# A convolution and a two-layer SiLU network on one Trainium2 core: the written-out order of a block, its table of PSUM banks and the list of the first blocks are laid out anew

## The chip, the core and the metric

The kernel runs on one NeuronCore of a Trainium2 chip. TensorE (PE) multiplies matrices into PSUM, which has eight banks of 128 x 512 float32. VectorE (DVE) and ScalarE (ACT) work on vectors, GpSimd (POOL) issues accumulating DMAs, and SyncE (SP) issues the other DMAs. The metric is the time of one execution on the device in microseconds. The kernel before takes 2326.64 us, the median of three runs (2324.93 to 2326.81).

## The reference, cut to what matters

```python
def _attn_ref(x, weight):                  # x: (8, 4096, 192), weight: (8, 7)
    w = softmax(weight, axis=-1)           # seven taps for each of 8 heads
    x_pad = concatenate([zeros((B, 6, D)), x], axis=1)
    x_unf = x_pad[:, idx, :].reshape(B, S, K, H, group)
    out = np.einsum('hk,bskhg->bshg', w, x_unf)   # causal convolution along S
    return out.reshape(B, S, D)

def _moe_ref(x, w_in, w_out):              # x: (32768, 192)
    h = x @ w_in                           # 192 -> 2048
    g = h * (1.0 / (1.0 + np.exp(-h)))     # SiLU
    return g @ w_out                       # 2048 -> 192
```

All of it is float32.

## The kernel before, in words

The 32768 tokens are cut into 32 blocks of 1024 (b = 0 to 31). Each block goes through these steps, and the kernel's text has a token for each:

- Loading and convolution, one block or two ahead. `ld.k` loads x (SP), `i.k` transposes it (DVE), `ha.0` sets the six columns of the block before (POOL and an SP DMA), `v.ki` is tap i of the channels k. Tap 0 is one ScalarE operation. For blocks above 3, each further tap is a ScalarE operation into a `u` buffer and a POOL DMA that adds it into `nat`; for blocks 1 to 3 it is one VectorE operation (line 517). `sp.k` copies the result into `dup` (SP), and `w.i` forms sums of it in `win` (DVE).
- The up stage. The first matrix product is done by a scheme with fewer multiplications than the plain one. `Pr.g` is product r (0 to 14) of group g (0 to 4), one matmul of 64 rows (line 650). The array is split into two halves of 64 rows, e=0 and e=1, and each product belongs to one half. `L.nk` are a few plain products (line 667). Between them a bank is read and written: `uo.g` copies a bank to a `u` buffer (ACT, line 699), `X`, `a` and `b` add or subtract (DVE, line 693), and `S` is the SiLU (ACT, line 711). So a product often waits for a copy or an add of a product a little earlier.
- The down stage. `t.ji` forms differences of SiLU outputs (DVE, 128 x 1024, line 734; t.j1 needs t.j0, t.j3 needs t.j1). `Di.je` is a slot: four matmuls of 32 columns side by side (line 766), for form i (0 to 5), hidden part j (0 to 3), half e. D0 and D1 read SiLU outputs alone; D2 also needs t.j1; D3 needs t.j2 and t.j3; D4 needs t.j0 and t.j3; D5 needs t.j3.
- The end of a block. `x`, `y`, `z` copy accumulators out of PSUM (ACT), `M` adds them (DVE), `o` transposes (DVE), `st` stores (SP).

The order of all this is written out in lists, and every engine does its instructions in the order of the list. `PLAN` holds the 300 tokens of one turn. A token's prefix says which block it is for: none for block b, `-` for b-1, `=` for b-2, `+` for b+1. (Loading and convolution tokens act on the block after the one so named.) PLAN is run for b = 3 to 33. `START` is one longer list that runs first and does the rest of block 0, and blocks 1 and 2; in it `dp` is the plain down stage of block 0 (line 787), `cp` its copies, and `go` starts GpSimd's combining of weights.

The banks are given by tables with rows for block 1, block 2 and all later blocks: `CHAIN_BANKS`, `XBANKS`, `PLAIN_BANKS` for the up stage, `ACC` for the accumulators of the down stage (one for each form 0 to 5; the seventh entry is for the second half of form 3 in the last block), and `DOWN_BANKS` for block 0.

In the last block, tokens in `held` are not done from the list: the t and D tokens of j = 2 and 3, and all of the end of the block. `finish()` does them afterwards in an order of its own. The t and D tokens of j = 0 and 1 are still done in PLAN's order.

`u` buffers are ten, handed out oldest-freed first; a convolution's buffer is free again when its DMA has landed. `t` tiles and the output tile share three buffers, and SiLU outputs have eight.

Of the kernel before, what the change touches and what calls it, by code (L numbers as in the profile page):

```python
# [17 lines left out]
def kernel(  # L18
# [60 lines left out]


    PLAN = (
# [20 lines left out]
    )  # L102
    START = (
# [41 lines left out]
    )  # L145
    QUEUE = (0, 4, 1, 2, 3)
    CHAIN_BANKS = (
# [3 lines left out]
    )  # L151
    XBANKS = (
# [3 lines left out]
    )  # L156
    PLAIN_BANKS = (
        (3, 4, 5),
        (7, 2, 1),
        (6, 1, 3),  # L160
    )
    ACC = (
        (3, 6, 4, 1, 5, 7, 5),
        (0, 3, 1, 2, 4, 6, 5),
        (6, 2, 3, 1, 4, 0, 5),
    )

    def pin(ins):
        return tc.keep_in_program_order(ins)
# [37 lines left out]
    x0 = x.flatten_outer_dims()[TB - pad : TB, :].rearrange("t (k c) -> c k t", k=NK)  # L207
# [565 lines left out]
                )  # L773
            )

    DOWN_BANKS = (7, 0, 2)

    def down_plain(b):

        cmbs[b] = [xpool.tile([P, 4, TB], F32, tag="cmb", name="cmb")]  # L780
        for j in range(NJ):
            for a in range(2):
                for e in range(2):
                    for k in range(NK):
                        for n in range(2):
                            pin(
                                nc.tensor.matmul(  # L787
                                    banks[DOWN_BANKS[k]][R * n : R * n + R, :],
                                    wo[j][:, a, e, R * k : R * k + R],
# [14 lines left out]
    def copy_plain(b, k):  # L804
        pin(nc.scalar.copy(cmbs[b][0][:, k, :], banks[DOWN_BANKS[k]]))

# [329 lines left out]
```

## Time and profile before

| what | value |
|---|---|
| median of 3 runs | 2326.64 us |
| profiled execution | 2326.81 us, its span 2325.1 us |
| PE, share of the span busy | 100% |
| DVE | 76% |
| ACT | 65% |
| POOL | 23% |
| granted clock of PE, mean | 0.999 |

"Busy" is the time in which an engine has at least one instruction under way, as the profiler records it. The stages alternate: an up stage, then a down stage, each about half of a block's time. A chain of waits is followed back from the last instruction; a piece such as "PE ps L766 x384" is a stretch in which it stays on matmuls of line 766. One matmul of float32 shows as two records, two passes, so 384 records are 192 matmuls, the 48 slots of a block. In the lists of instructions an entry in square brackets is the idle time of the engine before the instruction and what ended it.

### The profile page before, as it was taken

How to read it: one execution, taken by the hardware profiler on the slowest of the kernel's cores; microseconds unless marked ns; L12 is line 12 of the kernel's file. 1: busy time of each engine (PE TensorE's matmuls, PEld its weight loads, DVE VectorE, ACT ScalarE, POOL GpSimd, SP SyncE). 2: the span in 40 equal slices, each digit the busy share in tenths (PEclk: the TensorE clock that was granted, in tenths of full speed). 3: DMA queues.
4: the chain of work that ended last, by engine and by line, in shares of the span. 5: the costliest groups of instructions: out<-in, count | busy, mean ns of one | idle time of the engine just before them, and what ended most of it. 6: DMA issues, size and time to landing. Idle time of an engine off the chain costs nothing.

```text
span 2325.1 us, 45494 instructions
## 1 busy us (share of the span) xinstructions
PE 2315.7 (100%) x17630; PEld 978.7 (42%) x17630; DVE 1776.7 (76%) x2373; ACT 1505.4 (65%) x2779; POOL 535.9 (23%) x672
## 2 busy tenths in 40 slices
PE   9999999999999999999999999999999999999998
PEld 4344444344444344444444344444334453344443
DVE  8998877777777778777777777787777777777766
ACT  5347666677666676666776666766667766677642
POOL 4921122212122211222121221112221222212100
PEclk9999999999999999999999999999999999999999
DMA  7324566756566565666565675656666556756501
GB/s 159 67 53 87 100 103 114 126 103 113 91 121 120 105 112 96 112 114 122 103 109 94 119 125 101 116 94 115 114 118 107 102 98 119 123 102 107 88 16 18
DMA packets 523832, 238.80 MB, mean 103 GB/s; under 512 B 431648, under 2 KB 436768, under 8 KB 523616
## 3 DMA queue, kind: packets, MB, share of 16 engines
q0 software_dynamic: 73024, 133.73, 33.8%
q1 hardware_dynamic: 447392, 101.78, 24.3%
q8 instruction: 138, 2.26, 0.4%
q10 hardware_dynamic: 3200, 0.39, 0.1%
q14 instruction: 78, 0.64, 0.1%
HBM read 31.46 MB, written 25.17 MB: 24 GB/s over the span
## 4 chain that ended last, share of the span: by engine, by line
PE 99%; DVE 0%; ACT 0%; issue 0%; ACTq 0%
PE ps L766 48%; PE ps L650 45%; PE ps L667 2%; PE ps L787 2%; PE ps L589 2%; PE ps L1035 1%; PE ps L436 0%; DVE t L734 0%; DVE g L693 0%; DVE cmb L176 0%; ACT u L176 0%; DVE osb L176 0%; PE ps L462 0%; DVE zeros L176 0%; ACTq L969 0%
## 5 line engine op out<-in xcount | busy, mean ns | idle before, releaser
L513 POOL DMA_DIRECT2D nat<-u x504 | 430.9, 917 | 1556.7 <-ACT u L512 539.6
L650 PE MATMUL ps<-win,wr 64*128 64x512 f32 x1550 | 716.3, 591 | 0.0
L766 PE MATMUL ps<-g,wo 128*32 128x512 f32 x2976 | 677.1, 593 | 0.0
L650 PE MATMUL ps<-win,ws 64*128 64x512 f32 x1550 | 636.9, 592 | 0.0
L766 PE MATMUL ps<-t,wo 128*32 128x128 f32 (+2 forms) x4528 | 518.2, 447 | 0.0
L699 ACT COPY u<-ps 128x512 f32<-128x512 f32 x775 | 442.2, 589 | 117.1 <-PE ps L650 87.6
L766 PE MATMUL ps<-t,wx 128*32 128x512 f32 x2976 | 495.4, 592 | 2.2 <-DVE t L734 2.2
L512 ACT ACTIVATE u<-xt,taps 128x512 f32<-128x512 f32 x504 | 347.1, 724 | 166.1 <-DMA nat<-u 165.6
L734 DVE TENSOR_TENSOR t<-g 128x1024 f32<-128x1024 f32 x248 | 302.4, 1220 | 175.6 <-PE ps L766 175.6
L650 PE MATMUL ps<-dup,wr 64*128 64x512 f32 x868 | 422.5, 590 | 0.0
L734 DVE TENSOR_TENSOR t<-g,t 128x1024 f32<-128x1024 f32 x248 | 303.2, 1223 | 112.6 <-PE ps L766 106.1
L650 PEld LDWEIGHTS ps<-win,wr 64*128 64x128 f32 x1550 | 284.8, 187 | 201.6 <-issue 179.0
L711 ACT ACTIVATE g<-ps 128x512 f32<-128x512 f32 x465 | 268.1, 599 | 114.8 <-PE ps L650 106.7
L650 PEld LDWEIGHTS ps<-win,ws 64*128 64x128 f32 x1550 | 264.2, 186 | 163.9 <-issue 93.8
L693 DVE TENSOR_TENSOR g<-u,ps 128x512 f32<-128x512 f32 x465 | 309.3, 676 | 5.6 <-PE ps L650 5.3
L711 ACT ACTIVATE g<-g 128x512 f32<-128x512 f32 x465 | 277.9, 630 | 8.2 <-DVE g L693 8.2
L829 ACT COPY yx<-ps 32x512 f32<-32x512 f32 x150 | 86.9, 579 | 296.3 <-PE ps L766 294.9
L693 DVE TENSOR_TENSOR ps<-u,ps 128x512 f32<-128x512 f32 x310 | 211.8, 692 | 83.2 <-ACT u L699 62.4
L650 PE MATMUL ps<-dup,ws 64*128 64x512 f32 x682 | 269.8, 590 | 0.0
L766 PEld LDWEIGHTS ps<-t,wo 128*32 128x32 f32 x4528 | 179.6, 110 | 204.5 <-issue 201.3
L766 PE MATMUL ps<-g,wx 128*32 128x512 f32 x1488 | 246.6, 595 | 0.0
L766 PEld LDWEIGHTS ps<-g,wo 128*32 128x32 f32 x2976 | 170.9, 110 | 148.5 <-issue 139.1
(92 smaller groups left out, 1952.7 us busy)
## 6 DMA issues: line engine op xcount, KB each, us to landing
nat<-u POOLq DMA_DIRECT2D x504, 256.0 KB, 4.2
dup<-nat SPq DMA_DIRECT2D x345, 128.0 KB, 2.4
nat<-in_x_dram SPq DMA_DIRECT2D x382, 64.0 KB, 3.6
out_dram<-osb SPq DMA_DIRECT2D x376, 64.0 KB, 2.0
raw<-in_moe_w_out_dram SPq DMA_DIRECT2D x8, 384.0 KB, 4.0
raw<-in_moe_w_in_dram SPq DMA_DIRECT2D x12, 192.0 KB, 4.5
ws<-wr POOLq DMA_DIRECT2D x8, 192.0 KB, 5.0
raw<-in_moe_w_in_dram SPq DMA_DIRECT2D x6, 128.0 KB, 3.0
```

Of the source, the lines that this page charges most:

```text
L512: pin(nc.scalar.activation(z, src, AF.Copy, scale=tap))
L513: pin(nc.gpsimd.dma_start(out=dst, in_=z, accum_op=ALU.add))
L589: nc.tensor.matmul(hs[a, n, e], rows(wr[j], e)[:, a, k, :], rows(d, e)[:, n, k, :], start=k == 0, stop=k == NK - 1,)
L650: nc.tensor.matmul(to[:, cols], raw(g, *LEFT[e][r], e), rhs[:, cols], start=first, stop=True, skip_group_check=True,)
L667: nc.tensor.matmul(plain_bank(b, n and 1 + e)[:, cols], rows(wr[j] if own == e else ws[j], e)[:, a, k, :], rows(dups[b], e)[:, SLOT[e][2 * ...
L693: pin(nc.vector.tensor_tensor(out_, u, v, op=op))
L699: pin(nc.scalar.copy(us[b, g, o][:, cols], t1[:, cols]))
L711: pin(nc.scalar.activation(h, src, AF.Silu))
L734: pin(nc.vector.tensor_tensor(t[i // 2][:, i % 2, :], u, v, op=ALU.subtract))
L766: nc.tensor.matmul(accs[b][at][SQ * q : SQ * q + SQ, to], lhs[:, e, SQ * k : SQ * k + SQ], rhs[:, e, ts(q, TB // 4) if i == 5 else to], st ...
L787: nc.tensor.matmul(banks[DOWN_BANKS[k]][R * n : R * n + R, :], wo[j][:, a, e, R * k : R * k + R], gs[b, j, a][:, n, e, :], start=j == 0 an ...
L829: pin(nc.scalar.copy(to, acc[3 * (name[0] == "x") + k][n:P, :]))
```

## The change

PLAN has the same 300 tokens in another order, and the turn is cut at another place: 143 tokens now belong to the block before instead of 114, three (`o.2`, `st.2`, `st.3`) to the block before that, and `v.00`, `v.20`, `v.21` to the block after. START is written anew to fit, 549 tokens instead of 581. The rows of the bank tables for blocks 1 and 2 are new, and of those for all later blocks some entries. Nothing else changes; no function is touched. Cut to the places named below:

```diff
     PLAN = (
-        "+ld.1 -P14.3 -S3.3 -sp.0 -S4.3 P5.0 -P8.2 v.00 v.01 -a1.3 -S1.3 -S1.2 -b5.3 v.20 -t.00 "
-        "-P8.3 -a0.3 -t.02 P5.4 -S0.1 -D1.20 -sp.2 -D1.21 -S5.1 -t.01 -t.03 u5.0 -D1.10 -D0.31 "
-        "-D1.31 v.21 -D2.01 -D1.00 -a0.2 -D3.00 -D3.01 -D2.00 u5.4 -D4.00 -D5.00 v.10 v.11 "
...
+        "+ld.1 -P0.2 -u1.2 -X4.2 -P7.2 -P11.2 -S4.2 =o.2 =st.2 -a1.1 -S1.1 -P0.3 -P12.2 -X4.3 "
+        "-P7.3 v.01 -P11.3 -P12.3 -a5.2 -P4.2 -P14.2 -S4.3 -u1.3 -b1.2 -P10.2 -a5.3 -P8.1 -S5.0 "
+        "-S1.0 -a1.2 -S3.2 -P4.3 v.10 -P8.2 -P14.3 -S3.3 -b1.3 -a1.3 -P10.3 P5.4 -S5.1 v.11 "
+        "-P8.3 P5.0 v.02 -D1.00 =st.3 -t.00 -b5.3 -a0.2 -a0.3 -sp.2 -D1.30 u5.4 -a0.1 -D1.01 "
+        "v.22 v.12 -D0.00 -S0.3 v.23 -D0.31 -D1.10 -t.01 -t.03 -D2.00 -sp.0 -b5.2 -t.02 -D4.01 "
+        "-S1.2 -S5.2 -D5.00 -D2.01 v.03 -D5.01 -D3.00 -S0.1 -t.10 -D1.20 -D4.00 v.13 v.24 "
...
+        "-x2.1 -w.5 -x2.2 -D3.20 -x0.0 -D4.31 -D4.30 -M6.0 -M2.0 L.00 v.16 -M3.0 -M4.0 P2.0 "
+        "u4.0 P5.1 +i.1 L.10 u5.1 L.02 -M5.0 -o.3 -x1.0 P3.0 P6.0 u2.0 X2.0 P2.4 u4.4 -o.0 L.01 "
+        "SL.0 L.12 L.11 SL.1 +ld.0 P1.0 u0.0 SL.2 P9.0 P6.4 u2.4 P13.0 S2.0 X4.0 -M7.0 -st.0 "
+        "+i.0 P2.1 P3.4 X2.4 u4.1 P0.0 u1.0 P7.0 a5.0 P12.0 P11.0 S4.0 b1.0 P1.4 u0.4 P9.4 X4.4 "
+        "P4.0 P13.4 a1.0 P14.0 P10.0 b5.0 P7.4 a5.4 P0.4 S2.4 +ha.0 +v.00 S3.0 P6.1 P8.0 P3.1 "
+        "u1.4 u2.1 P11.4 a0.0 X2.1 P12.4 P4.4 a1.4 +v.20 b1.4 S4.4 S0.0 +v.21 P5.2 u5.2 P14.4 "
...
     START = (
...
+        "-D2.30 -x2.1 v.03 -x2.3 P2.0 u4.0 P3.0 -w.5 L.02 P2.4 u4.4 v.12 v.13 v.14 P6.0 u2.0 "
+        "v.15 v.25 v.26 v.04 -M1.0 -M2.0 -y2.0 L.00 +ld.0 -M6.0 L.01 SL.0 X2.0 P6.4 u2.4 -D4.30 "
+        "-D3.20 -D3.30 -M3.0 -x0.0 -D4.31 -x1.0 P9.0 P1.0 u0.0 -o.0 P13.0 S2.0 X4.0 P1.4 u0.4 "
...
     CHAIN_BANKS = (
-        ((1, 2, 4, 6, 6), (7, 0, 5, 1, 0), (6, 7, 7, 4, 5)),
-        ((2, 6, 5, 4, 0), (4, 0, 6, 1, 3), (1, 2, 3, 0, 7)),
-        ((5, 2, 5, 6, 7), (0, 4, 0, 3, 3), (1, 7, 1, 2, 0)),
+        ((4, 1, 2, 7, 7), (3, 4, 6, 5, 5), (1, 3, 3, 1, 0)),
+        ((0, 2, 5, 4, 6), (1, 6, 1, 0, 7), (5, 3, 2, 3, 0)),
+        ((5, 2, 5, 6, 7), (0, 4, 0, 3, 3), (1, 7, 2, 1, 1)),
     )
...
     ACC = (
-        (3, 6, 4, 1, 5, 7, 5),
-        (0, 3, 1, 2, 4, 6, 5),
-        (6, 2, 3, 1, 4, 0, 5),
+        (1, 2, 7, 4, 3, 5, 7),
+        (3, 4, 6, 1, 0, 2, 7),
+        (0, 6, 1, 3, 4, 2, 7),
     )
...
-    DOWN_BANKS = (7, 0, 2)
+    DOWN_BANKS = (0, 1, 5)
```

More of the change, by code (lines that the diff above doesn't have):

```diff
@@ L147 @@
     CHAIN_BANKS = (
[3 rows of a table removed]
[3 rows of a table added]
     )
     XBANKS = (
[3 rows of a table removed]
[3 rows of a table added]
     )
     PLAIN_BANKS = (
-        (3, 4, 5),
-        (7, 2, 1),
-        (6, 1, 3),
+        (0, 2, 1),
+        (5, 3, 4),
+        (6, 3, 1),
     )
     ACC = (
-        (3, 6, 4, 1, 5, 7, 5),
-        (0, 3, 1, 2, 4, 6, 5),
-        (6, 2, 3, 1, 4, 0, 5),
+        (1, 2, 7, 4, 3, 5, 7),
+        (3, 4, 6, 1, 0, 2, 7),
+        (0, 6, 1, 3, 4, 2, 7),
     )
```

109 rows, old and new, of tables (PLAN, START, XBANKS) are left out of this document.

## The prediction

> **What bounds the kernel now.** I read the page first: matmuls fill TensorE for 100% of the span, so nothing that frees another engine can pay unless TensorE waits somewhere. The chain of waits, in order of time, shows a block of the steady part:
>
> ```profile
> 2136.11 36.22 PE ps L766 x384
> ...
> 2177.26 30.11 PE ps L650 x139
> 2207.37 36.22 PE ps L766 x384
> ```
>
> Columns: start, length, what. From one down stage (L766) to the next is 71.26 us, and the chain never leaves PE in between. Next the table by stage (length, then busy time of PE, PEld, DVE, ACT, POOL, the granted clock, DMA share, GB/s):
>
> ```profile
> 2172.26:2207.30 35.04, 35.04 (x172) 17.74 (x168) 28.03 (x44) 27.25 (x52) 2.46 (x3) 1.00 0.39 69
> 101.55:139.76 38.21, 38.21 (x175) 20.28 (x173) 35.27 (x53) 28.52 (x55) 27.87 (x47) 1.00 0.29 49
> 175.97:211.45 35.48, 35.48 (x172) 17.66 (x168) 32.85 (x52) 26.15 (x50) 0.11 (x1) 1.00 0.23 40
> 2280.00:2282.00 2.00, 0.22 (x4) 0.16 (x8) 1.90 (x3) 0.74 (x2) 0.00 (x0) 1.00 0.00 0
> 2282.00:2284.00 2.00, 2.00 (x16) 0.48 (x12) 2.00 (x3) 0.32 (x1) 0.00 (x0) 0.74 0.00 0
> 2284.00:2286.00 2.00, 2.00 (x24) 1.09 (x20) 1.97 (x2) 1.88 (x4) 0.00 (x0) 0.50 0.00 0
> 2286.00:2288.00 2.00, 2.00 (x28) 0.87 (x24) 0.04 (x1) 0.00 (x0) 0.00 (x0) 0.90 0.00 0
> ```
>
> The first row is a steady up stage, the next two the up stages of blocks 1 and 2, the last four the beginning of the last block's down stage. The timeline of PE (start, length, engine, line, shapes) says what a steady up stage must cost and what happened at the end:
>
> ```profile
> 390.32 0.69 PE L650 MATMUL ps<-win,wr 64*128 64x512 f32 x1
> 390.33 0.69 PE L667 MATMUL ps<-dup,ws 64*128 64x512 f32 x1
> 390.85 0.59 PE L650 MATMUL ps<-win,wr 64*128 64x512 f32 x1
> ...
> 391.28 0.59 PE L650 MATMUL ps<-win,wr 64*128 64x512 f32 x1
> ...
> 2279.00 0.59 PE L766 MATMUL ps<-g,wo 128*32 128x512 f32 x1
> 2281.78 0.63 PE L766 MATMUL ps<-t,wx 128*32 128x512 f32 x3 [2.19 <-DVE t L734]
> ```
>
> A product runs as two passes, and the halves e=0 and e=1 run side by side. Passes of a half follow each other every 0.429 us. Each half has 78 full and 6 half-length passes (0.216 us): 33.46 + 1.30 = 34.76 us. At a change between products and slots a pass is 0.09 us late, three times a block: 0.28. Together 35.04, the measured row to the hundredth. The steady blocks have nothing to give. What can be won: up stage of block 1, 38.21 against a floor of 36.76 (two more products, all on e=1: 4 passes, 1.72); block 2, 35.48 against 35.04; and the hole at 2279.
>
> **The change, part by part.** No instruction is added or removed: both PLANs hold the same 300 tokens, so all work is the same and only order and banks differ. I counted positions in both lists.
>
> *The last block's down stage.* At the end, slots of j=2,3 are held for finish(), so only slots of j=0,1 run, and the cover is thin. Now the order is D1.10, D2.01; D2.01 needs t.01. VectorE does, from the stage's start at 2278.53:
>
> ```profile
> 2278.77 0.68 DVE L693 TENSOR_TENSOR g<-u,ps 128x512 f32<-128x512 f32 x1
> 2279.37 1.22 DVE L734 TENSOR_TENSOR t<-g 128x1024 f32<-128x1024 f32 x1
> 2280.51 2.55 DVE L734 TENSOR_TENSOR t<-g,t 128x1024 f32<-128x1024 f32 x2
> ```
>
> that is a0.3, t.02, then t.01 and t.03. t.01 ends at 2281.73, and TensorE, which could have gone on at 2279.42, starts at 2281.78: 2.36 us lost. The table shows what follows: clocks of 0.74, 0.50 and 0.90, so half speed for 1.04 + 2.00 + 0.40 = 3.4 us, which costs another 1.71. Together 4.07. In the new list four slots that need no t come first, D1.00, D1.01, D0.00, D1.10: 4 x 0.858 = 3.43 us. VectorE does a0.3 from +0.24 (as above), a0.1, t.01, t.03, b5.2, t.02: t.01 starts at 0.24 + 0.60 + 0.60 = 1.44 and ends at 2.66, before D2.00 at 3.43; t.03 ends at 1.44 + 1.14 + 1.22 = 3.80, before D4.01 at 4.29; t.02 ends at 5.5, before D3.00 at about 6.4. The hole goes, and with it the half clock: **-4.07**. Late next would be t.03, by 0.5 us of margin.
>
> The half clock's price can be weighed. The row: 2.2 us of idle PE, then 3.4 us at half clock. The Trainium skill, page "TensorE: Matmul & The Clock Gate", section "HAM oscillation", puts the danger at idle gaps over about 3.4 us. By that rule this gap would be harmless and the part worth 2.36, a sum 1.7 us higher; the trace shows a throttle after a shorter gap, so the row decides.
>
> *Steady blocks.* Here only a loss is possible. I compared each hand-over: products between the one that fills a bank and the one that waits for its reader, against the readers' time. The form with least room is product, u copy, X add, product two places on: 2 x 0.858 = 1.72 us of products against 0.2 (matmul's tail) + 0.59 + 0.05 + 0.70 + 0.05 = 1.58. The old list has it at P9 of groups 0, 2 and 3, beside three like it (u copies or b adds before P1.3, P10.0, P12.4); the new one has it twice (P9.0, P13.2), the rest have 0.35 or more. Since the old list runs at the floor with more such places, I cost the steady up stages at **0**, and the down stages too (36.22 in both: same slots, banks are read by copies with more room). Some old stages ran longer (35.17, 35.33, two by a few hundredths, 0.5 us in all); I take back **-0.3**, with 0 and -0.8 as ends.
>
> *Work moved across the block's cut.* v.00, v.20, v.21 now go into the up stage of the block before, behind ha.0. ScalarE does its queue in order, so a late halo would hold S3.0, u1.4, u2.1 behind it. Room: i.0 follows X4.0, which follows P9.0. From P9.0's end: 0.2 + 0.60 (X4) + 0.60 (M7) + 0.70 (i) + 0.05 + 1.9 (halo's median landing by its line) = 4.05. v.00 comes after S2.4, which needs P13.4, six products of its half later: 5.15 + 0.2 + 0.52 = 5.87. Margin 1.8 us, so 0. SyncE's stores =st.2, =st.3 move from before the cut to after it; the buffer they free is wanted again by t.10, some 7 us behind =st.3, against 2.0 us to landing: 0.
>
> *START and banks.* Block 1: between its first product and first slot VectorE has 35.8 us of work in the old list and 33.1 in the new one (13 convolution adds become 11, two transposes one, two t one, one b less, two w more; spacing 0.87, 0.70, 1.14, 0.60 by their rows). It is the engine that TensorE waited for there, so I take 37.1, nearest to the floor: **-1.1** (ends -1.45 and 0). Block 2: four slots of block 1 (D4.30, D3.20, D3.30, D4.31) now stand amid its products, one more pair of changes: +0.28. P9.0 then waits for X2.0, which stands behind w.5, seven convolution adds, M1, M2, M6: 0.60 + 7 x 0.75 + 1.80 + 0.70 = 8.35, while TensorE comes to P9.0 after 4 products, 4 slots and the changes, 7.1. If VectorE starts that late the wait is 1.2; it can start before, in the down stage: I take 0.5. 35.04 + 0.28 + 0.5 against 35.48: **+0.3** (ends -0.2 and +1.4). Block 3: by the new ACC of block 2 its slot 4 lies in the bank that P3.0 of block 3 opens, and x1.0, the last reader, stands behind u5.1: 0.18 + 1.72 + 0.2 + 0.48 + 0.65 = 3.2, while P3.0 could go at 2.3: **+0.9** (0 to 0.9). DOWN_BANKS: the down stage of block 0 ran 41.35 without a gap and its banks are free in time; 0.
>
> **Sum** against the profiled execution's 2326.81 (its span of 2325.1 and 1.7 around it, untouched): -4.1 - 0.3 - 1.1 + 0.3 + 0.9 = -4.3, so **2322.5 us**, that is 4.1 below the median of 2326.64, which differs little from it. About 0.2%, 4.7 us, is what a measurement of this kernel can tell from no change; the forecast lies just inside.
>
> **Rivals.**
> - *START at its floor.* Waits for X2.0 and x1.0 vanish, block 1 at 36.8, the odd longer stages too: -4.1 - 0.8 - 1.45 - 0.2 = -6.5, 2320.3. For it: TensorE has often a few passes in hand. Against: VectorE is 92% busy there. 0.22.
> - *The tail stays.* Another input comes late (a0.3 must wait for the very last product) and the hole only moves, the clock falls all the same: 2326.81 - 0.2 = 2326.6. Against: 0.5 us of margin at the closest. 0.09.
> - *Slower: the halo blocks ScalarE.* Place: +v.00 behind +ha.0 in each up stage. It decides when the chain of 4.05 us takes over 5.87, say a halo landing in 3.7 instead of 1.9; that line's longest landing was 3.5 (before the steady part). Each microsecond beyond costs 28 blocks x 1 us; 0.3 us gives 2322.5 + 8.4 = 2330.9, 0.5 us 2336.5. For it: SP must issue it behind loads and stores. 0.12.
> - *Order of products.* If products ran strictly as listed, each starting after the one before it has begun, counting both lists by halves gives an up stage of 35.7 for the old and 35.3 for the new: 28 x 0.43 = 12 us less, 2310.5. Against it the rows at 390: the list has P2.0, P2.4 (both e=1), then L.00 (L667, e=0), and L.00 starts 13 ns after P2.0, ahead of P2.4; and 35.04 is below 35.7. 0.02. The same page, "Step-by-step: what each phase is for", says that matmuls stay in program order and only weight loads are pulled ahead; this trace does not agree for matmuls on different rows of the array.
>
> **How the numbers follow.** Forecast 0.55, spread 2321 to 2325 by START's ends; a fifth of it lies below 2322.0. Faster: 0.22 + 0.02 + 0.10 = 0.34. Slower (over 2331.3): most of the halo's 0.12, 0.10. Within: 0.56. The range leaves out the order rival and most of the halo rival: 2320.2 to 2328.0.
>
> **What would show it.** Right: no PE wait on t in the table of waits; clock 1.00 over the last down stage; steady stages 35.04 and 36.22; down stage of block 1 beginning near 138.6, that of block 3 within 1 us of 282.7. Wrong: steady up stages above 35.1, ScalarE idle before L509 in them, or a clock below 1.00 before the last stores.

## The result and the profile after

The kernel after takes 2320.19 us, median of 11 runs (2319.66 to 2321.2), against 2326.28 us for the kernel before in the same comparison (11 runs, 2324.8 to 2326.81). The ratio is 0.9976, with a 95% interval of 0.9966 to 0.9985: by the medians 6.1 us or 0.26% faster, a small gain but clear of no change, where 4.1 was forecast. The time lies at the very edge of the range, whose low end is 2320.2.

I compared the two profiled executions by the starts of their stages. Their spans are 2325.1 and 2318.0, so there are 7.1 us to find.

| stretch | before | after | change | forecast |
|---|---|---|---|---|
| up to the up stage of block 1 | 101.55 | 101.02 | -0.5 | 0 |
| up stage of block 1 | 38.21 | 36.93 | -1.28 | -1.1 |
| down stage 1 with up stage 2 | 71.70 | 71.73 | +0.03 | +0.3 |
| up stage of block 3 | 35.04 | 36.09 | +1.05 | +0.9 |
| a usual up stage of blocks 4 to 31 | 35.045 | 34.97 | 28 x -0.075 = -2.1 | 0 |
| the odd longer ones among them | +0.47 | +0.24 | -0.2 | -0.3 |
| a steady down stage | 36.22 | 36.22 | 0 | 0 |
| last down stage to the end of the span | 46.58 | 42.45 | -4.13 | -4.07 |

I take the first line as variation: the thirteen profiles of both kernels and of their variants spread there by 0.7 us, and the kernel before alone gives 101.55 and 101.02 (e5, below). An odd longer stage is one that takes some tenths more than its neighbours. These are the rows of the table by stage (length, busy time of PE, PEld, DVE, ACT, POOL, granted clock, DMA share, GB/s) for the kernel after: the up stages of blocks 3 and 1, a steady one, and the beginning of the last down stage, which starts at 2275.51.

```profile
245.90:282.00 36.10, 35.25 (x173) 16.28 (x169) 27.36 (x42) 29.32 (x55) 2.55 (x3) 1.00 0.43 74
101.02:137.95 36.93, 36.93 (x175) 27.41 (x173) 33.69 (x51) 28.28 (x53) 26.97 (x47) 1.00 0.29 51
2169.36:2204.33 34.97, 34.97 (x172) 16.59 (x168) 26.28 (x40) 26.81 (x50) 0.86 (x1) 1.00 0.30 53
2276.00:2278.00 2.00, 2.00 (x24) 0.62 (x20) 2.00 (x4) 1.15 (x2) 0.00 (x0) 1.00 0.04 8
2278.00:2280.00 2.00, 2.00 (x24) 0.72 (x20) 1.97 (x3) 0.00 (x0) 0.00 (x0) 1.00 0.00 0
2280.00:2282.00 2.00, 2.00 (x37) 0.84 (x31) 1.92 (x3) 1.67 (x4) 0.00 (x0) 1.00 0.00 0
```

In the last three rows PE is full and its clock is 1.00; before, one slice had 0.22 of 2.00 busy and the next three had clocks of 0.74, 0.50 and 0.90. In the first row PE lacks 0.85 us. The waits of PE in the kernel after (what waited, for what, us in total, times, longest) name it:

```profile
PE ps L435 <- DVE warm L175: 1.1, 1, 1.1
PE ps L649 <- ACT yx L828: 0.8, 1, 0.8
PE ps L461 <- DVE wown L175: 0.2, 1, 0.2
```

No wait for a t tile is left. The one new wait behind the start of the program is that for x1.0 of block 2 (line 828; the lines of the kernel after are one lower than before). PE's timeline at that place, and ScalarE's:

```profile
247.73 0.59 PE L666 MATMUL ps<-dup,ws 64*128 64x512 f32 x1
249.17 0.69 PE L649 MATMUL ps<-win,wr 64*128 64x512 f32 x1 [0.85 <-ACT yx L828]
```

```profile
247.93 0.59 ACT L698 COPY u<-ps 128x512 f32<-128x512 f32 x1 [0.22 <-PE ps L649]
248.54 0.58 ACT L828 COPY yx<-ps 32x512 f32<-32x512 f32 x1
```

x1.0 could read its bank soon after the down stage (it starts at 246.16 in e2, below); here it stands behind the copy u5.1 in ScalarE's queue, which waits for P5.1. So it ends at 249.12, and P3.0 follows at 249.17.

### The profile page after: what moved, and what is told of

The parts are those of the page before. It is cut to its first block, busy times and chain, and to the rows that moved or that the text cites. A ratio compares the mean times of both kernels' runs of the same rounds, so it can differ in the third digit from the quotient of the medians.

```text
span 2318.0 us, 45422 instructions
## 1 busy us (share of the span) xinstructions
PE 2309.5 (100%) x17630; PEld 950.3 (41%) x17630; DVE 1797.6 (78%) x2373; ACT 1496.6 (65%) x2779; POOL 530.8 (23%) x672
## 4 chain that ended last, share of the span: by engine, by line
PE 89%; DVE 0%; ACT 0%; issue 0%; ACTq 0%
PE ps L765 45%; PE ps L649 39%; PE ps L666 5%; DVE cmb L175 0%; ACT u L175 0%; DVE osb L175 0%; ACTq L968 0%; ACTq L175 0%
## 5 line engine op out<-in xcount | busy, mean ns | idle before, releaser
L765 PE MATMUL ps<-g,wo 128*32 128x512 f32 x2976 | 694.9, 592 | 0.0
L649 PE MATMUL ps<-win,wr 64*128 64x512 f32 x1550 | 688.7, 591 | 0.8 <-ACT yx L828 0.8
L649 PE MATMUL ps<-win,ws 64*128 64x512 f32 x1550 | 644.3, 589 | 0.0
L698 ACT COPY u<-ps 128x512 f32<-128x512 f32 x775 | 452.5, 588 | 163.4 <-PE ps L649 93.6
L765 PE MATMUL ps<-t,wo 128*32 128x512 f32 (+2 forms) x4528 | 538.5, 446 | 0.0
L765 PE MATMUL ps<-t,wx 128*32 128x512 f32 x2976 | 485.2, 592 | 0.0
L649 PEld LDWEIGHTS ps<-win,wr 64*128 64x128 f32 x1550 | 275.7, 187 | 217.0 <-issue 177.0
L710 ACT ACTIVATE g<-ps 128x512 f32<-128x512 f32 x465 | 281.1, 604 | 48.3 <-PE ps L649 46.8
L649 PEld LDWEIGHTS ps<-win,ws 64*128 64x128 f32 x1550 | 258.8, 187 | 125.9 <-issue 103.9
L831 ACT COPY cmb<-ps 96x512 f32<-96x512 f32 x30 | 17.5, 582 | 396.9 <-PE ps L765 396.9
```

The source lines that it names most:

```text
L649: nc.tensor.matmul(to[:, cols], raw(g, *LEFT[e][r], e), rhs[:, cols], start=first, stop=True, skip_group_check=True,)
L698: pin(nc.scalar.copy(us[b, g, o][:, cols], t1[:, cols]))
L710: pin(nc.scalar.activation(h, src, AF.Silu))
L765: nc.tensor.matmul(accs[b][at][SQ * q : SQ * q + SQ, to], lhs[:, e, SQ * k : SQ * k + SQ], rhs[:, e, ts(q, TB // 4) if i == 5 else to], st ...
L831: pin(nc.scalar.copy(c[0], acc[0][0:n, :]))
```

## The experiments

The first question was where the 2 us of the steady up stages come from, which I had put at 0. The second was whether each other term has the cause that I gave it.

**e1_tight: one old hand-over put back into the kernel after.** My theory after the result: the kernel before waits a little for one copy in each block, u2.3 between P6.3 and P1.3, with only P1.2 of that half between them. Rival: the gain comes from the order as a whole.

```diff
-"... u2.2 P3.2 P6.3 P10.1 S1.4 a5.1 P3.3 u2.3 P14.1 S3.1 X2.2 P1.2 P13.2 S2.2 P9.2 u0.2 P4.1 b5.1 X2.3 P13.3 P1.3 ..."
+"... u2.2 P3.2 P14.1 S3.1 P10.1 S1.4 a5.1 P6.3 P3.3 u2.3 X2.2 P1.2 P13.2 S2.2 P9.2 u0.2 P1.3 P4.1 b5.1 X2.3 P13.3 ..."
```

> The kernel after, with one hand-over made as tight as it stood in the old list: P14.1 goes ahead of P6.3, and P1.3 ahead of P4.1, so that only one product (P1.2) of its half lies between P6.3 and P1.3, which waits for the copy u2.3 in between. Theory (the steady gain of 0.07 us a block is this one place going from one product of room to three): the steady up stage goes from 34.97 to about 35.05 us, and the run is some 2 us over the kernel after, about 4 us under the kernel before. Rival (the gain comes from the order of the halves at the stage's start, or from the DMAs that land with more room): the up stage stays at 34.97, and the run is within 0.5 us of the kernel after.

Measured: 2326.56 us, ratio to the kernel before 1.0001 (0.9992 to 1.001), the steady up stage 35.20. The place decides, but it cost 0.23 a block, three times what I had expected. Counting the passes of each half shows why: P1.3 starts 0.12 late, its own first pass then lasts 0.104 longer, and a first pass on the other half does the same 0.7 us later. 28 x 0.23 = 6.4 us; that this is about as much as the whole change gains is chance, since the edit made the place tighter than it had been in the kernel before.

The kernel before shows the milder form. Its PE timeline, then ScalarE's, in a steady block:

```profile
486.59 0.59 PE L650 MATMUL ps<-win,ws 64*128 64x512 f32 x1
487.01 0.67 PE L650 MATMUL ps<-win,ws 64*128 64x512 f32 x1
...
487.52 0.59 PE L650 MATMUL ps<-win,ws 64*128 64x512 f32 x1
```

```profile
486.35 0.58 ACT L699 COPY u<-ps 128x512 f32<-128x512 f32 x1 [0.26 <-PE ps L650]
```

The copy ends at 486.93 and the product starts at 487.01, on time (0.42 after the pass before it), but its first pass lasts 0.67 instead of 0.59 and the next starts 0.51 later instead of 0.43. P1.3 adds into the bank that u2.3 copies, so what came just in time is the bank. No idle time shows, so neither the table of waits nor the chain has it: it is in the spacing of the passes alone.

**e9_before_loose: the same place loosened in the kernel before.** The counterpart of e1.

```diff
-"... P10.1 S5.4 b5.1 P14.1 S3.1 sp.1 P3.3 P6.3 u2.3 P9.2 P8.1 P1.2 P13.2 X4.2 X2.3 P1.3 P9.3 P11.2 ..."
+"... P10.1 S5.4 b5.1 P6.3 u2.3 P14.1 S3.1 sp.1 P3.3 P9.2 P8.1 P1.2 P13.2 X4.2 X2.3 P1.3 P9.3 P11.2 ..."
```

> The kernel before with the one tight place of its half e=1 loosened: P6.3 and u2.3 of PLAN stand ahead of P14.1 instead of behind it, so that two products of that half, P14.1 and P1.2, lie between P6.3 and P1.3, which waits for u2.3. Theory (the old steady up stage held a wait of 0.08 at this place): the up stages become 34.97 as in the kernel after, about 27 x 0.075 = 2.0 us in all, 2324.3, while the hole before the last down stage stays as it was. Rival (the gain lies elsewhere, in the order as a whole): 35.04 as before, 2326.3.

Measured: 2340.21 us, ratio 1.006 (1.0045 to 1.0075), 13 us slower than the kernel before. Both expectations missed. The waits of PE have a new line, 28 times 0.19 us. The timelines of one block, PE, ScalarE and VectorE:

```profile
991.70 0.69 PE L650 MATMUL ps<-win,ws 64*128 64x512 f32 x1 [0.19 <-DVE ps L693]
```

```profile
989.73 0.60 ACT L711 ACTIVATE g<-ps 128x512 f32<-128x512 f32 x1 [0.27 <-PE ps L650]
```

```profile
990.36 1.29 DVE L693 TENSOR_TENSOR ps<-u,ps 128x512 f32<-128x512 f32 x2 [0.70 <-ACT g L711]
```

P14.1 is one product later, so S3.1, which reads its result (by the order of the list it is the line of ScalarE above), ends at 990.33. X4.2 starts at 990.36: by the bank tables it writes bank 2, and S3.1 is the last reader of bank 2 (chain 0 of group 1). X2.3 stands behind X4.2 on VectorE and ends at 991.65; P9.3 starts at 991.70, and P11.2 of the other half, listed behind it, goes with it at 991.71. The up stage is 35.53, 28 x 0.49 = 13.7 us. The tight place is gone, and a wait two engines away took its place: order and bank table belong together, and here the place could not be loosened alone. So this run does not confirm the 2 us in the kernel before; they rest on the spacing of the passes in both kernels and on e1.

**e6_before_pad and e7_after_pad: VectorE made longer.** A rival for the steady gain: the new order leaves more room to VectorE's adds in general. Both kernels got a `memset` of 128 x 1 (59 ns by its row) behind each X, a and b.

```diff
+    pad_op = const.tile([P, 1], F32, name="pad_op")
...
+            vec.memset(pad_op, 0.0)
```

> The kernel before with one tiny extra VectorE operation (a memset of 128x1) behind each X, a and b add, 35 a block; the outputs stay the same. It lengthens VectorE's queue by some 0.06 us at each hand-over, which is what the search held in hand. Theory (the old order's up stage lives with one hand-over of one product and several with under 0.2 us of room): its steady up stage grows from 35.05 by 0.2 us or more, and the run by 6 us or more. Rival (VectorE has room enough in both orders, it is busy for 28 of 35 us): the steady up stage stays within 0.05 us.

> The kernel after with the same tiny extra VectorE operation behind each X, a and b add. Theory: the new order holds this in hand nearly everywhere (two places with 0.14 us, the others 0.35 or more), so its steady up stage stays at 34.97 to 35.05 and the run grows by under 3 us, most of it in START, where VectorE is 92% busy. Rival: it grows as much as the kernel before does.

Measured: 2326.84 (ratio 1.0004, 0.9995 to 1.0014) and 2320.52 (0.9977, 0.9968 to 0.9986). The block of the kernel before grows from 71.26 to 71.29, that of the kernel after stays at 71.19, as expected. What I expected of the kernel before (0.2 a block) was wrong: room of 0.06 us on VectorE hardly tells the orders apart.

**e10_before_halves and e11_after_halves: the copies made longer.** The tight place waits for a ScalarE copy, which the memset does not lengthen. So each u copy was split into two of 256 columns.

```diff
-            pin(nc.scalar.copy(us[b, g, o][:, cols], t1[:, cols]))
+            m = (cols.start + cols.stop) // 2
+            for c in (slice(cols.start, m), slice(m, cols.stop)):
+                pin(nc.scalar.copy(us[b, g, o][:, c], t1[:, c]))
```

> The kernel before with every u copy (L699) done in two ScalarE instructions of 256 columns, so that its reader gets it later: by the row of 256 columns (366 ns) twice against 589, 0.14 us later. Theory (the margin of the copies separates the two orders): the place before P1.3, late by 0.08 already, gets later by 0.14 and by a late first pass of 0.10, about 0.24 a block, and the other three places of 0.13 room begin to wait: the up stage 35.3 to 35.6, the time 2333 to 2342. Rival (TensorE has the same room in both orders): both kernels of this pair grow by the same.

> The kernel after with every u copy (L698) done in two ScalarE instructions of 256 columns, 0.14 us later for its reader. Theory: only two places (P9.0, P13.2) have as little room as 0.13, so at most 0.01 of wait and its late first pass each: the up stage 34.97 to 35.2, the time 2320 to 2326, and it grows by less than half of what the kernel before grows by with the same edit. Rival: both grow by the same.

Measured: 2328.86 (ratio 1.001, 1.0001 to 1.0019) and 2322.27 (0.9981, 0.9971 to 0.999). The two copies of a pair overlap, so a pair takes 0.65 against 0.59, and the reader gets its data 0.06 later, not 0.14. The usual up stages become 35.11 and 35.02, +0.06 and +0.05, so the kernel before missed its expected 35.3 to 35.6, and the rival is right that both grow by about the same. In the kernel before, the place of P1.3 turns from 0.08 into a start 0.04 late and a first pass 0.10 longer; in the kernel after, a place early in the stage that had been on time gets 0.05. So the new order isn't safer against longer copies by this size; it has no place that was late already. Whether it bears a larger lengthening better was not tried.

**e2_x1_early and e8_x1_m5_early: the wait of block 3.** In e2 x1.0 stands ahead of P2.0 instead of behind u5.1; in e8 M5.0 stands ahead of the transpose as well.

```diff
-"... L.00 v.16 -M3.0 -M4.0 P2.0 u4.0 P5.1 +i.1 L.10 u5.1 L.02 -M5.0 -o.3 -x1.0 P3.0 ..."
+"... L.00 -x1.0 v.16 -M3.0 -M4.0 P2.0 u4.0 P5.1 +i.1 L.10 u5.1 L.02 -M5.0 -o.3 P3.0 ..."       e2
+"... L.00 -x1.0 v.16 -M3.0 -M4.0 P2.0 u4.0 P5.1 -M5.0 L.10 u5.1 L.02 +i.1 -o.3 P3.0 ..."       e8
```

> The kernel after, with x1.0 moved from behind u5.1 to right behind L.00. Theory (block 3's P3.0 waits for x1.0 of block 2, since there alone they share a bank): the up stage of block 3 falls from 36.09 to about 35.0 us, all later ones stay at 34.97, and the run is 1.1 us under the kernel after, about 2319.1. Rival (ScalarE is what is late there, whatever comes first; then u4.0 is late instead and P6.0 waits): that stage stays over 35.6, or every later up stage grows by some tenths, which would cost 28 times as much and more than undo it.

> The kernel after with x1.0 right behind L.00 as in the run before, and M5.0 moved ahead of u5.1, with i.1 behind it. M5.0 is VectorE's read of the same bank and was the 0.5 us wait that took the place of x1.0's. Theory: the up stage of block 3 falls to about 35.05 us, the later ones stay at 34.97, and the run is 1.1 us under the kernel after, near 2319.1. Rival (yet another reader is late): that stage stays over 35.5.

Measured for e2: 2319.82 us (ratio 0.9972, 0.9961 to 0.9983), the up stage of block 3 35.74, so only 0.35 of the 1.05 came back. x1.0 now ends at 246.74, but its bank has a second reader, M5.0. PE's timeline and VectorE's in e2:

```profile
248.95 0.66 PE L649 MATMUL ps<-win,wr 64*128 64x512 f32 x1 [0.50 <-DVE cmb L843]
```

```profile
248.16 0.65 DVE L843 TENSOR_TENSOR cmb<-cmb,ps 96x512 f32<-96x512 f32 x1
```

Measured for e8: 2318.99 us (2318.59 to 2319.52; ratio 0.9972, 0.9961 to 0.9983). The stage is 35.12, and of PE's waits one is left, at the start of the program:

```profile
PE ps L435 <- DVE warm L175: 1.1, 1, 1.1
```

So the +1.05 was x1.0 and, behind it, M5.0. The median of e8 is 1.2 us below that of the kernel after and the lowest measured. The intervals of the two ratios overlap; what the traces show is the stage, 36.09 and then 35.12.

**e3_t02_late and e4_slot_ahead: the tail of the kernel before.** e3 moves t.02 behind t.01 and t.03; e4 also puts D1.00 ahead of D2.01.

```diff
-"... -P8.3 -a0.3 -t.02 P5.4 ... -t.01 -t.03 u5.0 -D1.10 -D0.31 -D1.31 v.21 -D2.01 -D1.00 ..."
+"... -P8.3 -a0.3 P5.4 ... -t.01 -t.03 -t.02 u5.0 -D1.10 -D0.31 -D1.31 v.21 -D2.01 -D1.00 ..."       e3
+"... -P8.3 -a0.3 P5.4 ... -t.01 -t.03 -t.02 u5.0 -D1.10 -D0.31 -D1.31 v.21 -D1.00 -D2.01 ..."       e4
```

> The kernel before, with t.02 moved behind t.01 and t.03. Theory (the hole in the last down stage is D2.01 waiting for t.01, one t operation too late): the hole shrinks by one operation's 1.14 us, from 2.2 to about 1.1 us of idle time. What the clock does after so short a hole no run has shown: if it falls all the same, the run is 1.1 us under the kernel before; if it stays at 1.00, 2.8 us under. Rival (another input of that slot is late too): the hole keeps its 2.2 us and the time is the same.

> The kernel before, with t.02 moved behind t.01 and t.03, and D1.00 ahead of D2.01. Theory: two slots without t stand ahead, 1.7 us, and t.01 is done 2.06 us into the stage, so the hole falls to about 0.3 us, the clock stays at 1.00, and the run is about 3.7 us under the kernel before. All other stages as in the kernel before (up stage 35.05, block 1's 38.2). Rival (the half clock at the end does not come from the hole): the run gains only 2 us, and the clock still falls in the last down stage.

Measured: 2324.69 (ratio 0.9993, 0.9984 to 1.0001) and 2324.77 (0.9994, 0.9985 to 1.0003). The times alone can hardly be told from no change; the traces can. From the last down stage to the end both take about 44.5 instead of 46.58. PE's timeline, e3 then e4:

```profile
2280.53 0.63 PE L766 MATMUL ps<-t,wx 128*32 128x512 f32 x3 [1.05 <-DVE t L734]
2283.00 1.93 PE L766 MATMUL ps<-t,wo 128*32 128x256 f32 x32 [0.54 <-DVE t L734]
```

```profile
2280.17 0.63 PE L766 MATMUL ps<-t,wx 128*32 128x512 f32 x3 [0.19 <-DVE t L734]
2282.63 1.94 PE L766 MATMUL ps<-t,wo 128*32 128x256 f32 x32 [1.40 <-DVE t L734]
```

In e4 the hole that I aimed at is nearly gone, but D3.00 needs the t.02 that I had moved back: 1.59 us idle in both. What is gained is the clock, which stays at 1.00 (1.7 us), and 0.4 us by the shorter hole. Only the whole reordering of the kernel after, with four slots of SiLU outputs ahead and t.02 before D3.00 by more slots, closes it. The expectations of e4 (-3.7) and of e3 with the clock at 1.00 (-2.8) were wrong for that reason: by the medians both gained 1.8.

**e5_before_look: the kernel before once more, as it is.**

> The kernel before as it is, for a second profile. Theory: steady up stages 35.04 to 35.05, and the hole before D2.01 of the last block about 2.2 us long again. Whether the clock falls after it is open: if the fall depends on where the hole lies in the time over which the clock is decided, it may stay at 1.00 here, and the run is then 1.7 us shorter; if every such hole brings it, the last down stage loses 4.1 us once more.

Measured: 2325.2 us, span 2323.5. PE's timeline has the same hole, but the clock stays at 1.00 and the stretch to the end is 44.88:

```profile
2281.87 0.63 PE L766 MATMUL ps<-t,wx 128*32 128x512 f32 x3 [2.18 <-DVE t L734]
```

Five profiles have a hole of 2.2 us there (the kernel before twice, e6, e9, e10). In four the clock falls and the stretch is 46.45 to 46.62; in this one it doesn't, and 1.6 to 1.7 us are saved. So the half clock follows such a hole mostly, not always.

The traces show what tells them apart. They hold the moments at which the granted clock changes. In the kernel before it rises at 6.29 us, falls at 2282.97, rises at 2286.39 and falls at 2323.93, and these moments lie 667, 1 and 11 steps of 3.413 us apart; in each of the thirteen profiles all changes lie on such a grid. In the four profiles with the fall, one step of the grid holds 2.19 (the kernel before), 1.92 (e6), 2.15 (e9) and 2.16 us (e10) of idle PE, and the clock falls at the end of that step. In e5 the grid cuts the hole in two, 1.42 us in one step and 0.76 in the next, and in e3 and e4 no step holds more than 1.05. So what goes with the fall is the idle time within one step, with the limit somewhere between 1.42 and 1.92 us. Where the steps lie against the kernel's start differs from one execution to the next. This is read from the traces; no run was aimed at it.

## Why the prediction was right, and where not

**The tail, -4.07.** Right in size and cause: -4.13, no wait for t, clock 1.00. The margin was thinner than I wrote. VectorE in the kernel after:

```profile
2275.43 1.87 DVE L692 TENSOR_TENSOR g<-u,ps 128x512 f32<-128x512 f32 x3
2277.22 2.48 DVE L733 TENSOR_TENSOR t<-g,t 128x1024 f32<-128x1024 f32 x2
```

Three adds come first where I counted two, so t.01 starts 1.71 after the stage's start (forecast 1.44) and t.03 ends at 2279.70, 4.19 after it, while D4.01 goes at 4.32: 0.13 of margin, not 0.5. And by e5 the part of it that is clock, 1.7 us, is not paid in each execution of the kernel before.

**The Trainium skill's rule on the clock.** The rule that I weighed (page "TensorE: Matmul & The Clock Gate", section "HAM oscillation": gaps over about 3.4 us are the danger) would have made this part 2.36. The profiled pair gave 4.13, and the measurement decides: 2.2 us of idle PE were enough in four profiles of five, at least 1.92 of them within one step, and the holes of e3 and e4 (1.05 and 0.54, 0.19 and 1.40) did not lower the clock.

**The steady blocks, 0.** This is the term that I mis-sized: it is -2.1 us. The failed step is "at a change between products and slots a pass is 0.09 us late, three times a block: 0.28. Together 35.04 ... The steady blocks have nothing to give". I had fitted the floor to the row. The passes of each half show two late ones at a change (0.09 to 0.12 at the first pass of the stage, 0.09 at its end), and a third in the middle of the stage that belongs to no change: the first pass of P1.3, 0.08. Without that third one, 34.76 with about 0.10 at the first pass and 0.09 at the end makes 34.95, within 0.02 of the row after, 34.97. e1 shows that this hand-over can cost that and more. My count of hand-overs had named "u copies or b adds before P1.3" among the close ones and set them at 0, because a sum came out to the hundredth.

**Block 1, -1.1; block 2, +0.3; block 3, +0.9.** They came to -1.28, +0.03 and +1.05. In block 1 the size was near, but by luck, for the reason was another: I had put TensorE's wait down to VectorE and its amount of work. PE's timeline at the beginning of the stage, with a line of ScalarE, in the kernel before, and then PE's in the kernel after:

```profile
101.55 1.98 PE L650 MATMUL ps<-dup,wr 64*128 64x512 f32 x4
103.35 1.55 PE L650 MATMUL ps<-win,wr 64*128 64x512 f32 x5
102.70 0.58 ACT L699 COPY u<-ps 128x512 f32<-128x512 f32 x1
```

```profile
101.02 0.69 PE L649 MATMUL ps<-dup,wr 64*128 64x512 f32 x1
101.03 0.69 PE L666 MATMUL ps<-dup,ws 64*128 64x512 f32 x1
```

The four passes at 101.55 are P5.0 and P5.4, both on half e=1. Half e=0 stands empty until P3.0 at 103.35, 1.8 us into the stage. P3.0's own bank had been copied out by 100.55, but ahead of P3.0 in the list stands P2.0, which waits for the copy u5.0, done at 103.28. In the kernel after, L.00 on e=0 starts together with P5.0. If the passes are given to the halves in the order of the list, the late starts of e=0 in this stage add up to 3.37 us before and 2.08 after, 1.29 less, which is the change. No run alters this place alone.

Block 3 went as worked out: x1.0 behind u5.1, then P3.0; e2 adds that M5.0 would have been next, by 0.5. In block 2 the change of stages is paid (the two pieces, 3.73 and 31.65, together are 35.38), but P9.0 doesn't wait for X2.0: no such wait of PE is in the table, and P9.0 opens the second piece right behind the slots, so the 0.5 that I took for it was not due. The -0.3 for odd stages came out as -0.2, but says little: these stages add up to 0.47 in the kernel before and to 1.1 in its second profile (e5), to 0.24 in the kernel after and to nothing in e2.

**The rivals.** *START at its floor* gave 2320.3, next to the time, but not by its mechanism: x1.0 did make P3.0 wait and block 1 gave 1.28 of 1.45; the missing 2 us came from the steady blocks. *The tail stays* did not happen, though by 0.13 us of margin. *The halo* holds nothing up: its longest landing is 2.9 us, ScalarE does not wait for it in the steady part, and the steady stage became shorter. *Order of products* asked for an up stage below the old one by 0.43; it is 0.07. Two places show something near it, though. In e9 P11.2 on one half started only with P9.3 on the other, which was listed ahead of it and waited; in block 1 of the kernel before P3.0 stood behind P2.0 in the same way. So in these places a product did not pass one of the other half that waited for another engine, while L.00, in the rows at 390, did pass P2.4, which only waited for its turn on its own half.

**The sum.** -4.3 was forecast for the profiled execution and -7.1 found; the difference is mainly 2.1 in the steady term, 0.5 of variation ahead of block 1 and 0.3 in block 2. The medians differ by 6.1. That the time still falls at the edge of the range is luck: the low end had been drawn for the rival in which START reaches its floor, and what brought the time there was the steady term, which no rival had at that size.

## What to carry to other kernels

A stage that agrees with a sum to the hundredth isn't at its floor if one term of the sum was fitted to it: count late passes one by one, since a product whose bank comes free just in time shows no wait but a longer first pass, and here 0.07 us in each of 28 blocks was a third of the gain. Judge a written-out order together with its bank table: moving one product by one place freed one hand-over and cost 13 us through the last reader of a bank (e9), and moving one copy uncovered the next reader of the same bank (e2). Where the array works in two halves, look at each half by itself: the chain says that PE is busy while one half stands empty behind the other's wait (block 1). At the end of a program, where work is held back, check separately what covers each wait.

## What the runs showed of the hardware that was not expected

- P1.3, a product of 64 rows whose bank came free 0.08 us before its start, has a first pass of 0.67 us instead of 0.59 (the kernel before). After a real wait of 0.12 the first pass is 0.104 longer (e1), about as much as at a change of stage (0.10 to 0.11).
- A hole of 2.2 us in PE's work halved the granted clock for 3.41 us in four profiles of five. In the four at least 1.92 us of it lay within one step of the 3.413 us grid on which all changes of the clock lie; in the fifth the grid cut it into 1.42 and 0.76.
- Two ScalarE copies of 256 columns in a row take 0.65 us together, though each lasts about 0.38 (the median of the rows): they overlap, and splitting a copy of 0.59 costs only 0.06 (e10).
